# Computing the normaliser z of a linear-attention block inside the G stage, in front of its last group, with the zeroing of a buffer on GpSimd

## The chip, the cores and the metric

The kernel runs on one core of a Trainium2 chip. The metric is the device time of one execution in microseconds (us), lower is better. Engines in the profiles: PE is the matmul engine (PEld its weight loads), DVE the vector engine, ACT the scalar engine, POOL is GpSimd, SP issues DMAs.

## The reference

Two blocks in parallel on one layer-normed input: linear attention (A) and a dense GELU layer (B).

```python
def _A_ref(x, wqkv, wo):                 # x: 1 x 2048 x 640, H = 32 heads of 20
    q, k, v = ...                        # x @ wqkv, split
    phi = lambda t: jnp.where(t > 0, t + 1, jnp.exp(t)) + 1e-6
    pq, pk = phi(q), phi(k)
    kv  = jnp.einsum("bhsd,bhse->bhde", pk, v)
    z   = jnp.einsum("bhsd->bhd", pk)                 # sum over tokens
    num = jnp.einsum("bhqd,bhde->bhqe", pq, kv)
    den = jnp.einsum("bhqd,bhd->bhq", pq, z)[..., None] + 1e-6
    return (num / den -> b s d) @ wo
# out = x + A(layernorm(x)) + B(layernorm(x)),  B(x) = gelu(x @ w1 + b1) @ w2 + b2
```

## The kernel before

The kernel keeps everything on chip. Its stages on PE, in order, are: hidden layer of B; k (16 token tiles); G = xn^T PK (five groups); q chunk 0; z; KVT (masked kv, from G); q chunks 1 and 2; M (KVT times wo); q chunk 3; the den matmuls; and the output. z is used only through ZB, and ZB only by the den matmuls. KVT and G reuse the memory of W1.

A small planner records each instruction with what it reads and writes, and puts in the semaphore waits. It hands each engine its instructions in the order in which they are recorded, so an instruction that waits holds up what is recorded behind it (in z_before_4th below PE stands 3.20 us in front of z and does not take the G matmuls behind it first). PSUM, where the results of PE land, is used as eight banks, handed out round-robin by `take(n)`.

```python
def phi(src, b, nb, dst, res_dst, extra_w):     # src: a PSUM bank (or pair) just filled by PE
    ... # ACT:  e2 = exp(src)                                              (L463)
    ... # DVE:  et = min(et, 1) + 1e-6                                     (L464)
    ... # DVE:  dst = max(src, 0) + e2      -> this frees the PSUM bank    (L466)

for t in range(NT):      # k stage: 10 matmuls of 320 columns, then phi -> PK[:, t, :]
    ...

Pl.ins(v, lambda e: e.memset(KVT, 0.0), writes=[r_KVT] + r_W1)             # v is DVE
for f in range(DT):      # G: 5 groups of 32 matmuls
    b = take(2)
    for t in range(NT):
        ... # PE: bank(b + h) += xn_tm[:, t, f]^T PK[:, t, half h]         (L487)
    ... # ACT: GTb[:, f, :] = bank pair

Pl.ins(v, lambda e: e.tensor_tensor(out=zsum, in0=PK[:, 0, :], in1=PK[:, 1, :], op=ALU.add), ...)
for t in range(2, NT):   # token sum, fp32, on DVE                          (L497)
    ...
# zhl = bf16 high part and bf16 low part of zsum, DVE                       (L500, L501)

def z_step():
    b = take(1)
    ... # PE: 10 matmuls of ONE column: bank(b)[:, j] = zhl[:, i, j::5]^T ones   (L517)
    ... # DVE: z_sb = bank(b)                                               (L521)
    for j in range(DT):  # DVE: ZB[:, j, :] = bmask * z_sb[:, j]            (L523)
        ...

def kvt_step():          # per t: 5 matmuls (L529), then DVE: KVT block = bank * maskKV[t]  (L533)
    ...
def m_step():
    for j in range(DT):
        b = take(2)
        ... # PE: 16 matmuls on 32 columns of KVT each                      (L545)
        ... # ACT: Msb[:, j, :] = bank pair                                 (L550)

q_chunk(0)               # q_chunk: 5 units of 5 matmuls of 512 columns (L509), each with phi -> PQ
z_step()
kvt_step()
q_chunk(1)
q_chunk(2)
m_step()
q_chunk(3)
```

## Time and profile before

The median is 210.89 us (210.71 to 210.95 over the first three runs); the profiled execution has a span of 209.0 us.

| engine | busy us | share of span |
|---|---|---|
| PE | 204.9 | 98% |
| DVE | 108.8 | 52% |
| ACT | 75.1 | 36% |
| POOL | 20.2 | 10% |

PE is nearly always busy. The way to find the rest is to look for the few places where PE stands still. This is the answer of the waits view of the kernel before, narrowed to PE and to the time from 98 to 131 us. Its columns are: engine and line that waited, whom it waited for, total us, how often, the longest.

```profile
PE ps L545 <- DVE PQ L466: 0.4, 2, 0.2
```

There is one such place: the M step (L545) waits twice for DVE to finish PQ (L466). A PQ instruction is the one that frees a PSUM bank of a q chunk, and the M step's banks are those that q chunk 2 used. So the M step waits for PSUM banks, because DVE empties them late. The timeline of the kernel before shows how late, and why. Its columns are: start, us, engine, line, operation, out<-in with shapes, count, and in brackets the idle time before it with its releaser.

```profile
99.10 0.82 DVE L501 TENSOR_TENSOR Msb<-Msb 128x640 bf16<-128x640 f32 x1
...
105.59 0.29 DVE L464 TENSOR_SCALAR ek<-ek 128x512 bf16<-128x512 bf16 x1 [5.67 <-ACT ek L463]
...
109.08 0.52 PE L517 MATMUL ps<-onesb,Msb 128*128 128x1 bf16 x10
...
110.92 0.15 DVE L521 COPY z_sb<-ps 128x5 f32<-128x5 f32 x1
...
111.11 1.31 DVE L523 TENSOR_SCALAR ZB<-bmask,z_sb 128x32 bf16<-128x32 bf16 x5
112.31 0.60 ACT L463 ACTIVATE ek<-ps 128x512 bf16<-128x512 f32 x1 [2.43 <-PE ps L509]
112.33 1.95 DVE L533 TENSOR_TENSOR W<-ps,maskKV 128x140 bf16<-128x140 f32 x5
...
114.20 0.28 DVE L464 TENSOR_SCALAR ek<-ek 128x512 bf16<-128x512 bf16 x1
...
121.91 1.29 PE L545 MATMUL ps<-Wo,W 128*32 128x320 bf16 x32
...
123.38 0.75 PE L545 MATMUL ps<-Wo,W 128*32 128x320 bf16 x16 [0.18 <-DVE PQ L466]
123.54 0.69 DVE L466 SCALAR_TENSOR_TENSOR PQ<-ps,ek 128x512 bf16<-128x512 f32 x1
...
124.38 1.29 PE L545 MATMUL ps<-Wo,W 128*32 128x320 bf16 x32 [0.24 <-DVE PQ L466]
...
125.60 4.73 PE L509 MATMUL ps<-xnT,Wqkv 128*128 128x512 bf16 x21
```

DVE does nothing between 99.92, when the low part of the token sum is done (99.10 + 0.82), and 105.59: it sat idle for 5.67 us. Then, just when q chunk 1 comes, it gets z_sb, ZB and the KVT masks one after the other. The first Exp of q chunk 1 is done on ACT at 112.91 (112.31 + 0.60), but DVE comes to it only at 114.20: a backlog of 1.29 us. From there DVE needs 0.995 us per unit and PE 1.08, so only 0.085 us is won back per unit. At the end of chunk 2 the backlog has not gone: the PQ of its last unit, from 123.54, frees the bank for the M step's last two pairs, which start at 124.38 after a wait of 0.24 us. In all the M step takes 3.69 us (from 121.91 to 125.60) instead of about 3.2.

The chain of waits of the kernel before (start, us, what):

```profile
60.38 21.73 PE ps L476 x160
...
109.24 0.36 PE ps L517 x10
...
206.68 0.29 DVE out_sb L656
```

From the first k matmul (60.38) to the last DVE instruction (206.68) are 146.30 us.

### The profile page before, as it was taken

Reading aid. Unit: us, or ns where it says so; the run is one execution under the profiler, and the core shown is the slowest. Engines: PE = TensorE matmul, PEld = TensorE weight load, DVE = VectorE, ACT = ScalarE, POOL = GpSimd, SP = SyncE. Lnnn points to the kernel's source line nnn. Section 1 sums busy time; section 2 is a strip of 40 time slices with the busy share of each in tenths; the row PEclk is TensorE's granted clock in tenths of the full one; section 3 lists DMA queues with packets and bytes.
Section 4 is the critical chain, followed back from the end, with each engine's and each line's share of the span. In section 5 each row is a group of like instructions: output and inputs, shape, how many; then the busy total and the mean of one; then the engine's idle time right before and its main releaser. Section 6 shows DMA issues by size and latency. Waiting matters only on the chain.

```text
span 209.0 us, 3950 instructions
## 1 busy us (share of the span) xinstructions
PE 204.9 (98%) x1599; PEld 141.0 (67%) x1599; DVE 108.8 (52%) x227; ACT 75.1 (36%) x142; POOL 20.2 (10%) x61
## 2 busy tenths in 40 slices
PE   7999999999999999999999999999999999999995
PEld 2799987444457777777756565577777777777775
DVE  4589970000008888999178975478633522523322
ACT  2689887666676444111253576100000000000000
POOL 3245568200000000000000000000000000000000
DMA  6999668997000000000000000591120111001001
GB/s 164 348 349 112 105 129 130 376 332 260 3 0 0 0 0 3 0 3 0 0 0 5 0 0 3 193 313 57 63 59 32 58 42 55 31 31 35 31 34 61
DMA packets 22507, 17.86 MB, mean 85 GB/s; under 512 B 9176, under 2 KB 22488, under 8 KB 22488
## 3 DMA queue, kind: packets, MB, share of 16 engines
q1 hardware_dynamic: 21808, 17.11, 29.1%
q10 hardware_dynamic: 680, 0.49, 0.9%
q8 instruction: 12, 0.20, 0.4%
q14 instruction: 7, 0.06, 0.1%
HBM read 12.62 MB, written 2.62 MB: 73 GB/s over the span
## 4 chain that ended last, share of the span: by engine, by line
PE 92%; DVE 6%; issue 1%; DVEq 0%
PE ps L617 33%; PE ps L355 25%; PE ps L487 10%; PE ps L476 10%; PE ps L509 5%; DVE PQ L466 3%; PE ps L298 2%; PE ps L653 2%; DVE ek L464 1%; DVE W L533 1%; PE ps L529 1%; PE ps L545 1%; DVE ZB L523 1%; PE ps L555 1%; PE ps L385 1%
## 5 line engine op out<-in xcount | busy, mean ns | idle before, releaser
L355 PE MATMUL ps<-xnT,W 128*128 128x128 bf16 (+2 forms) x435 | 52.0, 282 | 0.0
L617 PE MATMUL ps<-W,HG 128*128 128x320 bf16 x360 | 51.4, 299 | 0.0
L355 PEld LDWEIGHTS ps<-xnT,W 128*128 128x128 bf16 x435 | 35.6, 98 | 15.6
L617 PEld LDWEIGHTS ps<-W,HG 128*128 128x128 bf16 x360 | 35.1, 98 | 14.2 <-issue 0.4
L359 ACT ACTIVATE HG<-ps,b1c 128x128 bf16<-128x128 f32 (+2 forms) x87 | 40.1, 493 | 12.4 <-PE ps L355 10.3
L464 DVE TENSOR_SCALAR ek<-ek 128x512 bf16<-128x512 bf16 (+1 forms) x36 | 11.0, 305 | 42.7 <-ACT ek L463 41.6
L636 DVE TENSOR_TENSOR out_sb<-ps,xnT 128x640 bf16<-128x640 f32 x15 | 12.4, 825 | 36.2 <-PE ps L617 36.1
L463 ACT ACTIVATE ek<-ps 128x512 bf16<-128x512 f32 (+1 forms) x36 | 23.2, 645 | 20.4 <-PE ps L509 11.2
L617 PE MATMUL ps<-Msb,PQ 128*128 128x320 bf16 x150 | 22.5, 299 | 0.0
L509 PE MATMUL ps<-xnT,Wqkv 128*128 128x512 bf16 x100 | 22.1, 379 | 0.0
L476 PE MATMUL ps<-Wqkv,xnT 128*128 128x320 bf16 x160 | 21.9, 299 | 0.0
L487 PE MATMUL ps<-xPK,xn_tm 128*128 128x320 bf16 x160 | 21.9, 299 | 0.0
L476 PEld LDWEIGHTS ps<-Wqkv,xnT 128*128 128x128 bf16 x160 | 15.7, 98 | 6.2
L487 PEld LDWEIGHTS ps<-xPK,xn_tm 128*128 128x128 bf16 x160 | 15.7, 98 | 6.1
L617 PEld LDWEIGHTS ps<-Msb,PQ 128*128 128x128 bf16 x150 | 14.6, 98 | 5.7
L509 PEld LDWEIGHTS ps<-xnT,Wqkv 128*128 128x128 bf16 x100 | 11.6, 117 | 9.6 <-issue 0.2
L466 DVE SCALAR_TENSOR_TENSOR PQ<-ps,ek 128x512 bf16<-128x512 f32 x20 | 13.8, 692 | 2.1
L311 DVE BATCH_NORM_STATS2 stats<-xPK 128x6 f32<-128x320 bf16 x32 | 13.6, 466 | 2.3 <-DMA xPK<-in_A_x_dram 2.3
L466 DVE SCALAR_TENSOR_TENSOR xPK<-ps,ek 128x640 bf16<-128x640 f32 x16 | 13.2, 824 | 1.7
L497 DVE TENSOR_TENSOR Msb<-Msb,xPK 128x640 f32<-128x640 f32 x14 | 11.6, 825 | 0.5
L491 ACT ACTIVATE W<-ps 128x640 bf16<-128x640 f32 x5 | 3.5, 704 | 18.2 <-PE ps L487 14.6
L321 POOL TENSOR_TENSOR rstd<-aggr,mhalf 128x1 f32<-128x1 f32 x16 | 9.1, 568 | 8.9 <-DVE aggr L319 8.9
(68 smaller groups left out, 93.7 us busy)
## 6 DMA issues: line engine op xcount, KB each, us to landing
xnT<-in_A_x_dram SPq DMA_DIRECT2D x4, 640.0 KB, 6.2
Wqkv<-in_A_wqkv_dram SPq DMA_DIRECT2D x3, 800.0 KB, 6.7
out_dram<-out_sb SPq DMA_DIRECT2D x15, 160.0 KB, 1.8
W<-in_B_w_dram SPq DMA_DIRECT2D x1, 1920.0 KB, 15.3
W<-in_B_w_dram SPq DMA_DIRECT2D x3, 480.0 KB, 7.0
xPK<-in_A_x_dram SPq DMA_DIRECT2D x2, 640.0 KB, 9.5
Wo<-in_A_wo_dram SPq DMA_DIRECT2D x1, 800.0 KB, 10.5
xPK<-in_A_x_dram SPq DMA_DIRECT2D x4, 160.0 KB, 4.2
```

The lines of the kernel that those rows point to most:

```text
L311: Pl.ins(v, lambda e: e.bn_stats(stats[:, s, 6 * h:6 * h + 6], x_in[:, t, h * HW:(h + 1) * HW]), reads=[r_x[t]], writes=[r_stats[s][h]])
L355: Pl.ins("tensor", [(lambda e, k=k: e.matmul(bank(b, 0, w), W1[:, k, jb * P:(jb + 1) * P], xnT[:, k, tok], start=(k == 0), stop=(k == DT - ...
L359: Pl.ins("scalar", lambda e: e.activation(HG[:, jb, tok], bank(b, 0, w), ACT.Gelu_apprx_tanh, bias=b1c[:, jb:jb + 1]), reads=[B_[b], r_b1c ...
L463: Pl.ins("scalar", lambda e: e.activation(e2, src, ACT.Exp), reads=br, writes=[r_ek[s]])
L464: Pl.ins(v, lambda e: e.tensor_scalar(et, et, 1.0, 1e-6, ALU.min, ALU.add), reads=[r_ek[s]], writes=[r_ek[s]])
L466: Pl.ins(v, lambda e: e.scalar_tensor_tensor(out=d2, in0=src, scalar=0.0, in1=e2, op0=ALU.max, op1=ALU.add), reads=br + [r_ek[s]], writes= ...
L476: fns.append(lambda e, k=k, h=h, b=b, t=t: e.matmul(bank(b + h, 0, HW), xnT[:, k, t * P:(t + 1) * P], Wqkv[:, k, D + h * HW:D + (h + 1) * ...
L487: Pl.ins("tensor", [(lambda e, t=t, h=h, b=b, f=f: e.matmul(bank(b + h, 0, HW), xn_tm[:, t, f * P:(f + 1) * P], PK[:, t, h * HW:(h + 1) * ...
L497: Pl.ins(v, lambda e, t=t: e.tensor_tensor(out=zsum, in0=zsum, in1=PK[:, t, :], op=ALU.add), reads=[r_PK[t], r_zsum], writes=[r_zsum])
L509: Pl.ins("tensor", [(lambda e, k=k, j=j, b=b: e.matmul(bank(b), Wqkv[:, k, j:D:DT], xnT[:, k, cc], start=(k == 0), stop=(k == DT - 1))) fo ...
L617: return lambda e: e.matmul(bank(b + h, 0, HW), l, r[:, h * HW:(h + 1) * HW], start=(i == 0), stop=(i == JT + DT - 1))
L636: Pl.ins(v, lambda e: e.tensor_tensor(out=halves(out_sb[:, s, :]), in0=pair(b), in1=halves(x_res[:, t, :]), op=ALU.add), reads=B_[b:b + 2] ...
```

## The change

The intent: z's work goes to where DVE idles. For z to be ready in front of the fifth G group, the token sum has to begin earlier; so the zeroing of KVT, which stood in front of it on DVE, goes to GpSimd. z takes a bank out of turn (`zbank`), which also turns the bank order of everything behind it by one.

```diff
-        Pl.ins(v, lambda e: e.memset(KVT, 0.0), writes=[r_KVT] + r_W1)
+        Pl.ins(g, lambda e: e.memset(KVT, 0.0), writes=[r_KVT] + r_W1)
+
+        def z_step():
+            b = zbank
+            ...                       # otherwise as before
+        def token_sum():
+            ...                       # the same instructions as before
+        token_sum()
         for f in range(DT):
             b = take(2)
+            zbank = (b + 3) % 8
+            if f == DT - 1:
+                z_step()
             for t in range(NT):
...
-        Pl.ins(v, ... zsum ...)       # token sum and zhl behind the G loop: gone
...
         q_chunk(0)
-        z_step()
         kvt_step()
```

More of the change, by code (lines that the diff above doesn't have):

```diff
@@ L480, in bass_parallel_sum__linear_attn_block__dense_activation_gelu__prompt_kernel @@
             phi(pair(b), b, 2, PK[:, t, :], r_PK[t], [r_x[t]])
-        Pl.ins(v, lambda e: e.memset(KVT, 0.0), writes=[r_KVT] + r_W1)
+        Pl.ins(g, lambda e: e.memset(KVT, 0.0), writes=[r_KVT] + r_W1)
+        def z_step():
+            b = zbank
+            Pl.ins("tensor", [(lambda e, j=j, i=i: e.matmul(bank(b, j, j + 1), zhl[:, i, j:D:DT], onesb[:],
+                                                            start=(i == 0), stop=(i == 1)))
+                              for j in range(DT) for i in range(2)],
+                   reads=[r_zhl, r_small], writes=[B_[b]])
+            Pl.ins(v, lambda e: e.tensor_copy(z_sb[:], bank(b, 0, DT)), reads=[B_[b]], writes=[r_z])
+            for j in range(DT):
+                Pl.ins(v, lambda e, j=j: e.tensor_scalar(ZB[:, j, :], bmask[:], z_sb[:, j:j + 1], None, ALU.mult),
+                       reads=[r_z, r_bmask], writes=[r_ZB])
+        def token_sum():
+            Pl.ins(v, lambda e: e.tensor_tensor(out=zsum, in0=PK[:, 0, :], in1=PK[:, 1, :], op=ALU.add),
+                   reads=[r_PK[0], r_PK[1]], writes=[r_zsum])
+            for t in range(2, NT):
+                Pl.ins(v, lambda e, t=t: e.tensor_tensor(out=zsum, in0=zsum, in1=PK[:, t, :], op=ALU.add),
+                       reads=[r_PK[t], r_zsum], writes=[r_zsum])
+            Pl.ins(v, lambda e: e.tensor_copy(zhl[:, 0, :], zsum), reads=[r_zsum], writes=[r_zhl])
+            Pl.ins(v, lambda e: e.tensor_tensor(out=zhl[:, 1, :], in0=zsum, in1=zhl[:, 0, :], op=ALU.subtract),
+                   reads=[r_zsum, r_zhl], writes=[r_zhl])
+        token_sum()
         for f in range(DT):
             b = take(2)
+            zbank = (b + 3) % 8
+            if f == DT - 1:
+                z_step()
             for t in range(NT):
@@ L492, in bass_parallel_sum__linear_attn_block__dense_activation_gelu__prompt_kernel @@
                    reads=B_[b:b + 2], writes=[r_GT[f]] + r_W1)
-        Pl.ins(v, lambda e: e.tensor_tensor(out=zsum, in0=PK[:, 0, :], in1=PK[:, 1, :], op=ALU.add),
-               reads=[r_PK[0], r_PK[1]], writes=[r_zsum])
-        for t in range(2, NT):
-            Pl.ins(v, lambda e, t=t: e.tensor_tensor(out=zsum, in0=zsum, in1=PK[:, t, :], op=ALU.add),
-                   reads=[r_PK[t], r_zsum], writes=[r_zsum])
-        Pl.ins(v, lambda e: e.tensor_copy(zhl[:, 0, :], zsum), reads=[r_zsum], writes=[r_zhl])
-        Pl.ins(v, lambda e: e.tensor_tensor(out=zhl[:, 1, :], in0=zsum, in1=zhl[:, 0, :], op=ALU.subtract),
-               reads=[r_zsum, r_zhl], writes=[r_zhl])
         def q_chunk(c):
@@ L513, in q_chunk @@
                 phi(bank(b), b, 1, PQ[:, j, cc], r_PQ[c][j], [])
-        def z_step():
-            b = take(1)
-            Pl.ins("tensor", [(lambda e, j=j, i=i: e.matmul(bank(b, j, j + 1), zhl[:, i, j:D:DT], onesb[:],
-                                                            start=(i == 0), stop=(i == 1)))
-                              for j in range(DT) for i in range(2)],
-                   reads=[r_zhl, r_small], writes=[B_[b]])
-            Pl.ins(v, lambda e: e.tensor_copy(z_sb[:], bank(b, 0, DT)), reads=[B_[b]], writes=[r_z])
-            for j in range(DT):
-                Pl.ins(v, lambda e, j=j: e.tensor_scalar(ZB[:, j, :], bmask[:], z_sb[:, j:j + 1], None, ALU.mult),
-                       reads=[r_z, r_bmask], writes=[r_ZB])
         def kvt_step():
```

## The prediction

> What bounds it now. The page gives PE 98% busy; the chain of waits gives PE 92% of the span, DVE 6%. The PE timeline is dense: 160 G matmuls of 320 columns take 21.73 us (0.136 each), q matmuls of 512 columns 0.216 each. The waits view shows one place in the middle where PE stands still: the M step (80 small matmuls on KVT). In the stretch 121.9 to 125.7 PE is busy 3.38 of 3.80 us, with two waits for DVE's PQ evacuation (0.18 and 0.24). Its 32-matmul runs take 1.29 us, so 80 should take 3.23; from 121.91 to 125.67 they take 3.76. About 0.5 us is lost. Its PSUM banks are those of q chunk 2, which DVE empties late.
>
> Why DVE is late: after q chunk 0 it does z_sb, five ZB columns (1.50 us, 110.92 to 112.42, with gaps) and five KVT masks (to 114.28) before q chunk 1, whose first Exp was done at 112.91. It starts 1.3 us late. Then DVE needs 0.995 us per unit and PE 1.08, so it recovers only 0.085 us per unit, 0.8 over ten; the last unit ends at 124.24, 0.5 us later than without a backlog (Exp at 122.02 plus 0.60, 0.29, 0.69 and gaps: 123.74).
>
> What the change does.
> 1. It takes z_sb and ZB (1.50 us of DVE) out of this stretch, to about 99.5-101.5 us, where DVE would be idle until 105.6.
> 2. It takes the 1.39 us memset off DVE; the token sum starts 1.5 us earlier and zhl is done at about 98.5 instead of 99.92. The fifth G group starts at 82.1 + 4 x 4.35 = 99.5, so PE does not wait for zhl: margin 1 us. The memset's move serves this and saves nothing itself.
> 3. GpSimd zeroes 3200 bf16 columns. From its memsets of 140 and 512 columns (0.215 and 0.526 us) I estimate 2.9 us. It waits for PE's last use of W1, about 60.4, so runs to about 63.3; DVE is idle until 63.16. The Trainium skill, "SBUF — State Buffer", "Who interferes with whom", says that DVE's 2-port modes and GpSimd exclude each other; at most the k stage's first tensor_scalar waits some tenths, and DVE catches up (1.16 us per backlogged unit, PE 1.36). Not critical.
> 4. The 10 z matmuls stay on PE: 0.36 us in the chain before. Behind 320-column matmuls their weight loads (0.056 us each) hide less: estimate 0.45, so +0.1.
> 5. The bank order turns by one; z's bank was emptied long before. In the M step the first three pairs are then free, and the fourth waits for q chunk 2's last unit, about 123.8, just when PE arrives.
>
> On the critical path: -0.5 us (M step without waits) and +0.1 (z): about -0.4 us, 0.2%. Everything behind moves by that; no later stage has a PE wait that could grow.
>
> Predicted: 210.45 us, 8 in 10 between 210.0 and 210.85. Faster by over 2%: 0.5%; within 2%: 98.5%; slower: 1%.
>
> Seen in the profile if right: the M step's 80 matmuls in 3.2 to 3.35 us with no wait on DVE; DVE starts q chunk 1 within 0.4 us of its Exp; ZB at about 100 us; no PE gap ahead of the fifth G group; a GpSimd memset from about 60.5 of 2.5 to 3.5 us; k-stage and out-stage times unchanged.
>
> What would make it wrong: the GpSimd memset much longer, blocking DVE through the k stage so that PE or the z matmuls wait (slower by up to 1 us); z in front of G costing over 0.6 us; another wait behind the DVE one in the M step (no gain).

## The result, and the profile after

The median after is 210.34 us (210.04 to 210.70, six runs), against 210.87 us (six runs) before. The ratio is 0.9977, 95% interval 0.9964 to 0.9990: the change is clear of noise, but small, 0.2%. Ratios here are the mean time of one kernel's fast runs over that of the other's of the same rounds, so they are not quite the ratio of the medians quoted.

The waits view of the kernel after, asked for PE from 98 to 131 us in the same way, gives no line at all. The timeline of the kernel after, from which the zeroing (shown first) and the stretch around q chunks and M are taken:

```profile
60.72 2.77 POOL L483 MEMSET W<- 128x3200 bf16 x1 [22.39 <-PE ps L355]
...
63.34 0.33 DVE L464 TENSOR_SCALAR ek<-ek 128x640 bf16<-128x640 bf16 x1 [32.58 <-ACT ek L463]
...
97.66 0.83 DVE L504 TENSOR_TENSOR Msb<-Msb 128x640 bf16<-128x640 f32 x1
99.53 0.52 PE L488 MATMUL ps<-onesb,Msb 128*128 128x1 bf16 x10
...
100.28 1.31 DVE L494 TENSOR_SCALAR ZB<-bmask,z_sb 128x32 bf16<-128x32 bf16 x5
...
111.48 1.95 DVE L539 TENSOR_TENSOR W<-ps,maskKV 128x140 bf16<-128x140 f32 x5
112.49 0.60 ACT L463 ACTIVATE ek<-ps 128x512 bf16<-128x512 f32 x1 [2.04 <-PE ps L526]
113.35 0.28 DVE L464 TENSOR_SCALAR ek<-ek 128x512 bf16<-128x512 bf16 x1
...
122.10 3.26 PE L551 MATMUL ps<-Wo,W 128*32 128x320 bf16 x80
...
123.23 0.69 DVE L466 SCALAR_TENSOR_TENSOR PQ<-ps,ek 128x512 bf16<-128x512 f32 x1
...
125.29 5.59 PE L526 MATMUL ps<-xnT,Wqkv 128*128 128x512 bf16 x25
```

All 80 matmuls of the M step are now one unbroken row, and it takes 3.19 us (122.10 to 125.29) instead of 3.69. DVE comes to q chunk 1 at 113.35, 0.26 us after its Exp (113.09), not 1.29. The sum is ready at 98.49, 1.04 us before PE reaches z at 99.53. In the chain of waits of the kernel after, the marks are:

```profile
60.57 21.73 PE ps L476 x160
...
99.69 0.36 PE ps L488 x10
...
123.93 0.14 issue
124.07 1.29 PE ps L551 x32
...
206.37 0.29 DVE out_sb L661
```

From the first k matmul to the last DVE instruction: 145.80 us, exactly 0.50 less than before. This difference is cleaner than the times: the start of the k stage differs by some tenths between runs of one kernel (60.57 here, 60.23 in a second profile of the same kernel), because at the start PE waits for the first piece of W1. z costs 0.36 us in the chain in both places. The chain still passes through DVE and the M step (0.14 us of issue at 123.93), although PE shows no idle time there: DVE frees the last bank just when PE needs it. There is no room to spare.

### The profile page after: what moved, and what is told of

It is laid out like the page before. It is cut to its first block, busy times and chain, and to the rows that moved or that the text cites. A ratio compares the mean times of both kernels' runs of the same rounds, so it can differ in the third digit from the quotient of the medians.

```text
span 208.6 us, 3973 instructions
## 1 busy us (share of the span) xinstructions
PE 204.4 (98%) x1599; PEld 140.6 (67%) x1599; DVE 108.1 (52%) x226; ACT 74.9 (36%) x142; POOL 22.9 (11%) x62
## 4 chain that ended last, share of the span: by engine, by line
PE 92%; DVE 4%; DMA 3%; issue 0%; ACTq 0%; DVEq 0%
PE ps L622 33%; PE ps L355 25%; PE ps L514 10%; PE ps L476 10%; PE ps L526 7%; DVE PQ L466 3%; DMA W<-in_B_w_dram 3%; PE ps L658 2%; DVE ek L464 1%; PE ps L535 1%; PE ps L551 1%; PE ps L561 1%; PE ps L385 0%; PE ps L339 0%; ACTq L234 0%
```

## The experiments

Theory A is that of the prediction: the gain is the DVE queue freed of z_sb and ZB between q chunk 0 and the KVT masks, and the zeroing's move only makes it possible to have z that early. Rival B: taking 1.39 us off DVE pays. Rival C: the place of the z matmuls pays. Rival D: the turned bank order pays. The table gathers the results; "stretch" is the time from the first k matmul to the last DVE instruction in the chain of waits, worked out as above (the four-memset run is left out, since its chain starts elsewhere). Ratios are to the kernel before in the same rounds.

| run | median us | before, same rounds | ratio (95%) | stretch us | M step: PE waits for DVE |
|---|---|---|---|---|---|
| before | 210.89 | | | 146.30 | 0.4 us |
| after | 210.34 | 210.87 | 0.9977 (0.9964 to 0.9990) | 145.80 | none |
| memset_only | 210.88 | 210.89 | 1.0020 (0.9990 to 1.0049) | 146.32 | 0.4 us |
| z_moved_memset_on_dve | 211.20 | 210.89 | 1.0017 (1.0003 to 1.0031) | 146.48 | none |
| zb_late | 210.47 | 210.89 | 0.9980 (0.9966 to 0.9993) | 145.80 | none |
| zb_again | 211.16 | 210.89 | 1.0018 (1.0006 to 1.0031) | 146.50 | 0.8 us |
| old_bank_order | 210.33 | 210.83 | 0.9971 (0.9958 to 0.9985) | 145.80 | none |
| z_before_4th | 215.43 | 210.83 | 1.0215 (1.0198 to 1.0232) | 150.58 | none |
| memset_x4 | 213.70 | 210.83 | 1.0134 (1.0120 to 1.0148) | | none |
| z_high_only | 210.29 | 210.83 | 0.9969 (0.9957 to 0.9982) | 145.61 | none |
| after_again | 210.50 | 210.95 | 0.9986 (0.9972 to 0.9999) | 145.81 | none |
| z_high_only_again | 210.36 | 210.95 | 0.9969 (0.9956 to 0.9981) | 145.61 | none |
| zb_late_high_only | 210.27 | 210.95 | 0.9965 (0.9953 to 0.9978) | 145.61 | none |

All kernels gave the right result.

### memset_only: the zeroing alone

```diff
 # the kernel before
-        Pl.ins(v, lambda e: e.memset(KVT, 0.0), writes=[r_KVT] + r_W1)
+        Pl.ins(g, lambda e: e.memset(KVT, 0.0), writes=[r_KVT] + r_W1)
```

> The kernel before, with only the zeroing of KVT moved to GpSimd. Theory A (the gain is the DVE queue freed of z_sb and ZB between q chunk 0 and the KVT masks): the token sum ends 1.4 us earlier, at about 98.5, and nothing waits for it; the M step keeps its 0.5 us of waits; 210.9, ratio 0.999 to 1.001. Rival B (the 1.39 us taken off DVE is what pays): about 210.35, ratio 0.9975.

Measured: median 210.88 against 210.89, stretch 146.32 against 146.30; the M step keeps both waits. (One of its six runs took 212.75 us, which widens the interval of the ratio.) The long one had a mean granted clock of 0.992, where the other five had 1.0; it was not profiled, and why is open. Rival B falls: here the 1.39 us of DVE time, for which nobody waited, is worth nothing.

### z_moved_memset_on_dve: the move without the zeroing's move

```diff
 # the kernel after
-        Pl.ins(g, lambda e: e.memset(KVT, 0.0), writes=[r_KVT] + r_W1)
+        Pl.ins(v, lambda e: e.memset(KVT, 0.0), writes=[r_KVT] + r_W1)
```

> The kernel after, with the zeroing back on DVE. Theory A: zhl is done about 1.4 us later (98.5 to about 100.0) while PE wants it at 99.5, so PE waits about 0.5 to 0.6 us in front of the fifth G group, and the M step still runs in 3.2 us without waits: the gain is cancelled, 210.9 to 211.0, ratio 1.000 to 1.001. Rival C (the placing of z alone pays and the zeroing doesn't matter): 210.35, ratio 0.9975.

Measured: 211.20, ratio 1.0017. The timeline of this kernel, PE alone:

```profile
96.81 3.29 PE L514 MATMUL ps<-xPK,xn_tm 128*128 128x320 bf16 x23
100.57 0.56 PE L488 MATMUL ps<-onesb,Msb 128*128 128x1 bf16 x10 [0.47 <-DVE Msb L504]
...
123.17 3.27 PE L551 MATMUL ps<-Wo,W 128*32 128x320 bf16 x80
```

The M step is unbroken, as in the kernel after, but PE now stands 0.47 us in front of z. z itself takes 0.56 us in the chain here instead of 0.36: its first weight load starts at 100.56, behind the wait, where in the kernel after it starts at 99.39, while matmuls of G still run. Together that is 0.67, and the stretch is 0.68 longer than after. So the zeroing's move is worth nothing alone, and without it the rest of the change is worth less than nothing: the two belong together. Rival C's forecast for this run (210.35) fails too, but this alone does not settle it, since the wait could hide a gain; zb_late and zb_again below do.

### zb_late: only the ZB columns moved

```diff
 # the kernel before; the z matmuls, z_sb, bank order and zeroing stay
             Pl.ins(v, lambda e: e.tensor_copy(z_sb[:], bank(b, 0, DT)), ...)
+        def zb_step():
             for j in range(DT):
                 ... ZB[:, j, :] = bmask * z_sb[:, j]
...
         m_step()
+        zb_step()
         q_chunk(3)
```

> The kernel before, with only the five ZB columns moved on DVE, to behind the M step, where DVE idles; z matmuls, z_sb copy, bank order and the DVE zeroing stay where they were. Theory A: KVT masks end at about 113.0 instead of 114.3, the M step runs in 3.2 us, and the time equals that of the kernel after: 210.35, ratio 0.9975. Rivals B (zeroing off DVE), C (z matmuls in G) and D (the turned bank order) all expect no gain: 210.87, ratio 1.000.

Measured: 210.47, ratio 0.9980, stretch 145.80: to the hundredth that of the kernel after. The timeline of this kernel (PE and DVE):

```profile
113.43 0.28 DVE L464 TENSOR_SCALAR ek<-ek 128x512 bf16<-128x512 bf16 x1
...
122.11 3.26 PE L547 MATMUL ps<-Wo,W 128*32 128x320 bf16 x80
...
123.86 1.31 DVE L525 TENSOR_SCALAR ZB<-bmask,z_sb 128x32 bf16<-128x32 bf16 x5
```

This is the strongest of the runs. It has none of the three other parts of the change and has the whole gain, so rivals B, C and D are not needed to explain it. The five ZB instructions now run in the gap that DVE has while PE does M. (Its masks show a pause of 0.48 us between the second and third, which stays open; zb_late_high_only has one of 0.16 us in the same stage. The masks ended at about 113.5, not at the expected 113.0, and the M step still didn't wait.)

### zb_again: the old cost put back

```diff
 # the kernel after
         q_chunk(0)
+        zb_step()        # the five ZB instructions a second time, same values
         kvt_step()
```

> The kernel after, with the five ZB instructions done a second time in the old place, in front of the KVT masks (same values, so the result stays right). Theory A: 1.31 us of DVE work comes back; since z's matmuls no longer give DVE 0.36 us between q chunk 0 and the masks, the masks end at about 114.7, the backlog at q chunk 1 is about 1.6 us and after ten units at 0.085 us each still about 0.75 us; the M step takes about 3.9 us with a wait for DVE's last PQ: 211.1, ratio 1.001 (0.75 us above the kernel after, worse than before). Rivals B, C and D: as the kernel after, 210.35.

Measured: 211.16, ratio 1.0018; stretch 146.50, 0.70 above the kernel after. The timeline of this kernel, PE alone:

```profile
122.11 1.83 PE L556 MATMUL ps<-Wo,W 128*32 128x320 bf16 x48
124.78 1.29 PE L556 MATMUL ps<-Wo,W 128*32 128x320 bf16 x32 [0.83 <-DVE PQ L466]
```

With z's matmuls no longer behind q chunk 0, the same 1.31 us of DVE work hurts more than it did before (0.70 against 0.50). The reason given beforehand was that those matmuls had kept PE busy for 0.36 us while DVE emptied chunk 0; the backlog at q chunk 1 fits it: DVE comes at 114.58 to an Exp done at 113.10, 1.48 us late, against 1.29 in the kernel before. So a backlog of 0.26 us (after) cost nothing, 1.29 cost 0.50 and 1.48 cost 0.70 (0.75 expected): the DVE work in that place decides the M step's wait. The z matmuls stand in G here, and the gain is gone: with zb_late, rival C falls.

### old_bank_order: the bank order put back

```diff
 # the kernel after
         q_chunk(0)
+        take(1)          # skip one bank: every later bank is that of before
         kvt_step()
```

> The kernel after, with one bank skipped in front of the KVT step, so that every bank from there on is that of the kernel before. Theory A: the M step's third pair then waits for the fourth unit of q chunk 2 instead of the third, which is done in time, and the fourth pair for the fifth unit as it does now; no change, 210.35, ratio to before 0.9975, M step 3.2 us. Rival D (the turned bank order pays): 210.87, ratio 1.000.

Measured: 210.33, ratio 0.9971, stretch 145.80. Rival D falls.

### z_before_4th: z a whole group earlier

```diff
 # the kernel after
-            if f == DT - 1:
+            if f == DT - 2:
                 z_step()
```

> The kernel after, with z in front of the fourth G group instead of the fifth. The token sum should end at 98.5 as before and PE come to the z matmuls at about 95.2, so PE should stand still for about 3.4 us there: about 213.7, ratio 1.013. If PE could pass the waiting z matmuls, or the sum ended much earlier than the trace says, no loss: 210.35.

Measured: 215.43, ratio 1.0215, more than expected. PE waited about as long as expected, but the loss was 4.78 us of stretch against the kernel after. The timeline of this kernel, PE alone, and then the view of busy time by stretches (stretch, length, then busy us and counts of PE, PEld, DVE, ACT, POOL, then the granted clock, DMA share and GB/s):

```profile
98.25 0.56 PE L488 MATMUL ps<-onesb,Msb 128*128 128x1 bf16 x10 [3.20 <-DVE Msb L504]
98.67 10.22 PE L514 MATMUL ps<-xPK,xn_tm 128*128 128x320 bf16 x64
```

```profile
98.25:100.00 1.75, 1.75 (x16) 1.17 (x17) 1.01 (x5) 0.00 (x0) 0.00 (x0) 0.50 0.00 0
100.00:102.00 2.00, 2.00 (x11) 1.22 (x10) 0.32 (x2) 0.00 (x0) 0.00 (x0) 0.63 0.00 0
102.00:104.00 2.00, 2.00 (x17) 1.43 (x16) 0.00 (x0) 0.00 (x0) 0.00 (x0) 1.00 0.00 0
```

After a wait of 3.20 us the granted clock was 0.50, then 0.63, and only from about 102 us 1.00 again. In the chain the 64 matmuls behind the wait took 10.08 us, where at 21.73/160 us each they would take 8.69: 1.39 us lost to the clock, besides 3.20 of waiting and 0.20 for z. These make 4.79. The Trainium skill ("TensorE: Matmul & The Clock Gate", "What's actually happening") says that PE falls back to half its clock after an idle window of about 3.4 us and comes back after as long a busy time. The trace agrees in kind: all of the first 1.75 us and, by an average of 0.63, about three quarters of the next 2.00 us ran at half the clock, some 3.2 us together. The clock had fallen shortly before z began: asked for finer stretches, the same view gives 1.00 up to 98.00 and 0.63 from 98.00 to 98.25, so by this estimate about 0.2 us at half clock came before z, 3.4 us in all, and the fall came some 3.0 us after the last matmul had ended (95.05). It was no accident of one run: all four runs of this kernel had a mean granted clock of 0.992. The lesson for the change: of the places between G groups only the one in front of the fifth comes after the sum is ready; one group earlier costs about ten times what the change earns.

### memset_x4: GpSimd against DVE

```diff
 # the kernel after
-        Pl.ins(g, lambda e: e.memset(KVT, 0.0), writes=[r_KVT] + r_W1)
+        for _ in range(4):
+            Pl.ins(g, lambda e: e.memset(KVT, 0.0), writes=[r_KVT] + r_W1)
```

> The kernel after, with the GpSimd zeroing done four times, from about 60.7 to 71.9, so that three of them lie in the k stage where DVE works. If a GpSimd memset that only writes shuts DVE's two-port tensor_scalar out for its whole length, DVE gets about one of them in per 2.8 us, falls some 4 us behind, and PE stalls for up to 2 us: 211 to 212.5, with tensor_scalar waits of over 1 us. If it doesn't (in the trace after, a tensor_scalar that started 0.15 us before the memset ended took its usual 0.33 us), nothing changes: 210.35. I lean to the second.

Measured: 213.70, ratio 1.0134. My leaning was wrong. The timeline of this kernel (POOL, DVE and PE):

```profile
60.64 11.42 POOL L484 MEMSET W<- 128x3200 bf16 x4 [22.35 <-PE ps L355]
...
63.26 0.33 DVE L464 TENSOR_SCALAR ek<-ek 128x640 bf16<-128x640 bf16 x1 [32.56 <-ACT ek L463]
63.70 0.82 DVE L466 SCALAR_TENSOR_TENSOR xPK<-ps,ek 128x640 bf16<-128x640 f32 x1
64.44 2.03 DVE L464 TENSOR_SCALAR ek<-ek 128x640 bf16<-128x640 bf16 x1
...
66.57 0.82 DVE L466 SCALAR_TENSOR_TENSOR xPK<-ps,ek 128x640 bf16<-128x640 f32 x1
67.31 2.04 DVE L464 TENSOR_SCALAR ek<-ek 128x640 bf16<-128x640 bf16 x1
...
73.31 12.38 PE L476 MATMUL ps<-Wqkv,xnT 128*128 128x320 bf16 x90 [1.36 <-DVE xPK L466]
```

While the extra memsets run, each bf16 tensor_scalar (there are three) takes 2.03 to 2.04 us instead of 0.33, one for each extra memset; the scalar_tensor_tensor, which reads PSUM and one buffer, keeps its 0.82. DVE falls behind, PE waits three times for DVE in the k stage, 3.0 us in all by the waits view, and the loss is about 3.4 us (213.70 against 210.34). All of it lies in the k stage: in the chain it runs from 60.50 to 85.69, 25.19 us instead of 21.73, and from 60.50 to the last DVE instruction are 149.27 us, 3.47 more than after. The Trainium skill ("SBUF — State Buffer", "Who interferes with whom") says that DVE's 2-port modes and GpSimd share one pair of ports, and that one of them fully blocks for the length of the other's instruction; the trace agrees. In the kernel after there is no such loss because of timing alone: the single memset (60.72 to 63.49) lies where DVE has nothing to do, and the first tensor_scalar comes at 63.34. The 0.15 us by which the two overlap in the trace, from which I had leaned the other way, is no evidence; starts and ends of GpSimd work are rough there.

### z_high_only, and the second round: is PE's own work what is left?

```diff
 # the kernel after: z from the bf16 high part of the sum alone
-            ... zhl[:, i, j:D:DT], onesb[:], start=(i == 0), stop=(i == 1)) ... for i in range(2)
+            ... zhl[:, i, j:D:DT], onesb[:], start=True, stop=True) ...        for i in range(1)
-            Pl.ins(v, ... zhl[:, 1, :] = zsum - zhl[:, 0, :] ...)
```

> The kernel after, with z from the bf16 high part of the token sum alone: five z matmuls instead of ten and no zhl low part on DVE. Theory A says that after the change only PE's own work is left in this stretch, so the halved z (0.36 us in the chain) should give 0.18 us: 210.16, ratio 0.9966; the result stays right, as the 128 rounding errors of one column average out and ZB is bf16 anyway. If PE is still waiting somewhere for others, less or nothing: 210.35.

Measured: 210.29, ratio 0.9969, stretch 145.61: the trace shows 0.19 us less than after, but the kernel after was not timed beside it. So it was run again together with the kernel after, and with a third kernel that has zb_late's edit and this one on top of the kernel before.

> The kernel after, unchanged, as the measure for the two others on the same chip: 210.35, ratio 0.9975.

> The kernel with z from the high part alone, a second time, since in the first its trace showed 0.20 us less on PE but its time stood only 0.05 below the kernel after, which was not timed beside it. If PE's own work is all that is left here: 0.2 us below the kernel after of this call, 210.15, ratio 0.9966. If something behind it takes the time back: equal to the kernel after.

> Candidate for the best: the kernel before with the ZB columns behind the M step and z from the high part alone (z matmuls, zeroing and bank order in their old places). Theory A: no M step wait (0.5 us) and half of z's PE time (0.2 us): 210.15, ratio 0.9966, as the other high-only kernel. Its trace should show the z matmuls between q chunk 0 and the KVT step 0.2 us shorter and the M step in 3.2 us. If the placing of z in G had a worth of its own, it would stay above the other.

Measured: after 210.50, high part alone 210.36, ZB late with the high part alone 210.27. The two ratios of the high-only kernels, 0.9969 and 0.9965, lie below that of the kernel after, 0.9986, in the expected order of size, but the intervals overlap, so by time alone the further 0.2 us is not settled. The traces settle where it comes from: the stretch is 145.61 in all three profiles of high-only kernels, 145.80 and 145.81 in the two of the kernel after. So in this part PE's own work counts in full after the change: the halved z shortens it by 0.19. The lowest ratio is that of zb_late_high_only, 0.35% below before; by time it is not told apart from the other high-only kernel, and by the stretch they are equal. It leaves the zeroing, the token sum and the z matmuls where they were, and so has neither the 1 us margin nor the GpSimd memset to care for.

## Why the prediction was right

- What bounds it: right. The only idle time of PE in the middle was the M step's wait for DVE, and removing it gave 0.50 us by the trace (3.69 to 3.19), as predicted.
- Step 1, the DVE queue: right and shown from three sides. Moving ZB alone gives the whole gain (zb_late), putting it back takes it away (zb_again); the zeroing's move alone gives nothing (memset_only), and the bank order put back changes nothing (old_bank_order).
- Step 2, the margin: right. zhl was done at 98.49 (predicted about 98.5), PE came at 99.53 (99.5). With the zeroing back on DVE the margin turns into a wait of 0.47 us, and the gain into a loss.
- Step 3, GpSimd: the memset took 2.77 us (estimate 2.9) from 60.72. It cost nothing. That the two engines do exclude each other, which the prediction took from the skill, was shown by memset_x4. The harmlessness is one of timing.
- Step 4, z on PE: mis-sized. I expected z to cost 0.45 us in front of G instead of 0.36; it is 0.36 in the chain in both places. This is why 0.50 came out in the trace rather than 0.40; the time of 210.34 against 210.45 predicted fits it, though a difference of 0.1 is within the spread of single runs.
- Step 5, banks: right; the last pair's bank comes free just when PE arrives.

## What to carry to other kernels

When PE is 98% busy, look for the one stage where it waits, and follow that wait back through the engine's queue: here work that nobody needed for another 20 us stood in front of work that freed PSUM banks, and it only had to be recorded later. The engine behind was only 8% faster here than the one it serves, so its backlog lasted for ten units, and its effect showed far behind its cause. Before moving work to an earlier place, measure the margin there: a missed one cost the wait (0.47 us here, and 0.20 more for z), and where the wait was 3.20 us another 1.39 us for the clock.

## What the Trainium skill lacked or had wrong

- "SBUF — State Buffer", "Who interferes with whom": right about the exclusion, but it doesn't say how it looks in a profile. The blocked tensor_scalar is recorded as busy, 2.03 us instead of 0.33, not as idle; the memsets keep 2.77 to 2.83 us. Read by busy shares, DVE seems loaded where it is blocked. A memset on GpSimd, which writes only, is enough to block it.
- "TensorE: Matmul & The Clock Gate": it gives about 3.4 us of idle time for the fall to half clock. Here 3.20 us between matmuls (3.53 between weight loads) was followed by a granted clock of 0.50, and the fall came some 3.0 us after the last matmul had ended; a single such wait cost a further 1.39 us.
- "Perfetto Trace Analysis", "GPSIMD Engine Instruction": it says that instructions that read no tensor have only a single point in time reported. The memsets here have durations, 2.77 us for 3200 bf16 columns and 0.21 for 140, and four in a row fill 11.42 us.
- No page gives the time of a memset on GpSimd as such, only general rates per element: 2.77 us here for 3200 bf16 columns, which the kernel before zeroes on DVE in 1.39 us as 1600 uint32 words.
